# Two PSUM banks as two tiles instead of halves of one, in a fused attention and mixing kernel

## The chip, the core and the metric

The program runs on one core of one Trainium2 chip. The metric is device microseconds of one execution; lower is better.

## What is computed

A causal window attention (8 batches, 8 heads, 576 positions, 64 channels a head, window 128, a linear bias by distance) gives x, 8 batches of 576 x 512. Then each batch goes through a mixing layer:

```python
scores = scale * np.matmul(q, k.transpose(0, 1, 3, 2))
scores = np.where(mask, scores + bias[None], -1000000000.0)
attn = np.exp(scores - np.max(scores, axis=-1, keepdims=True))
attn = attn / (np.sum(attn, axis=-1, keepdims=True) + 1e-09)
x = np.matmul(attn, v)                      # then heads side by side: (8, 576, 512)
theta = x @ w_theta
y = np.einsum('ts,bsd->btd', w_tok_r, x * np.cos(theta)) + np.einsum('ts,bsd->btd', w_tok_i, x * np.sin(theta))
u = x + y
out = u + np.maximum(u @ w_ch, 0.0)
```

## The kernel before

The work is cut into steps. A step belongs to one engine and has an estimated cost; `Plan.__call__` notes which buffers it reads and writes. `Plan.order` simulates all steps with these costs several times, lets a list of numbers (`NUDGES`) disturb the priorities, and gives one fixed order. `Plan.run` emits the instructions in that order, so that every engine's queue, the DMA queue of SP among them, is laid out before the program runs. Where the plan leaves TensorE (PE) idle, `spin` fills the time with short matmuls on a constant tile (L365), whose result nobody reads.

Per pair of heads there are scores on PE (L613), a biased minimum on VectorE (DVE, L637), an exponential on ScalarE (ACT, L642), a transpose of the weights, and the product with the values (`attend`, L672). The first seven pairs (`early_pair`, L711) transpose their weights on PE into the tile `m_ps` (L720) and copy them out with ACT (L723); later pairs split them into two halves of 16 bits and transpose them by DMA. Then, per batch:

- `turn` (L748) computes theta (matmuls L793, L798 and L802 into the tiles `t_psa` and `t_psb`), sine and cosine (ACT, L824 and L826; the tables of sine and exponential are exchanged by a table load) and z = x cos, x sin in two parts of 16 bits.
- `mix` (L894) makes y: for two halves of the positions and four blocks of channels one group of 27 matmuls of 288 columns (L907), issued in three parts of nine, sums into one bank. DVE drains the bank into `xtf` (L913), ACT and DVE make u from that (L917, L920).
- `channels` (L925) multiplies u by w_ch: eight groups of 12 matmuls (L941) a batch, each drained by ACT with the ReLU (L951; tile `u_spare`), then added (L954 or L958) and written out (L960).

There are thus 64 groups of `mix` and 65 of `channels` (the last group of the last batch is cut in two). They take turns in two banks of PSUM. These banks are the two halves of one tile:

```python
a_ring, t_ring = banks("a_ps", 2), banks("t_ps", 2)      # L356: two tiles each
m_both = psum.tile([128, 2, 512], F32, name="m_ps")      # L357: one tile
m_ring = Ring([m_both[:, k] for k in range(2)])          # L358: its halves
```

The plan counts the halves as two buffers. The semaphores that the instructions wait for come from a layer below, which follows tiles. `t_psa` and `t_psb`, `a_psa` and `a_psb` are tiles of their own, used by the same rule of taking turns.

Of the kernel before, what the change touches and what calls it, by code (L numbers as in the profile page):

```python
# [52 lines left out]
while RAD * 0.5 > math.pi:  # L53
# [16 lines left out]
ROUNDS = 6  # L70
SELF = {"DVE": 0.115, "ACT": 0.13, "POOL": 0.1}
NUDGES = (
# [6 lines left out]
)  # L79


# [207 lines left out]
def attn_moe_kernel(ctx: ExitStack, tc: tile.TileContext, qt, kt, vx, wth, wtok, wch, band, out):  # L289
# [10 lines left out]
    def banks(name, n):  # L300
        return Ring([psum.tile([128, 512], F32, name=f"{name}{chr(97 + k)}") for k in range(n)])
# [51 lines left out]
    xp_ring = ring("xp", 2, [128, 2, 512], F16)  # L353

    s_ring = Ring([psum.tile([128, 2, 512], F32, name="s_ps")])
    a_ring, t_ring = banks("a_ps", 2), banks("t_ps", 2)  # L356
    m_both = psum.tile([128, 2, 512], F32, name="m_ps")  # L357
    m_ring = Ring([m_both[:, k] for k in range(2)])  # L358
    first_ring = ring("first", 2, [64, 2, 64], F32)

    def spin(tile, count):
# [240 lines left out]
    def scores(p, weights):  # L602
        qr, kr = raw_qk.pop(p)
        mx_buf, first = mx_ring.take(), first_ring.take()
        mx = mx_buf.tile.rearrange("p (e i) -> p e i", e=2)
        for group in range(2):
            ps, sb = s_ring.take(), sb_ring.take()

            def multiply(group=group, ps=ps):

                def part(e, at, q0, k0, kn, to):
                    rows = slice(64 * e, 64 * e + 64)
                    nc.tensor.matmul(ps.tile[at:at + 64, e, to:to + kn], qr.tile[rows, q0:q0 + 64],  # L613
                                     kr.tile[rows, k0:k0 + kn], start=True, stop=True)
                for j in range(2):
                    c = 2 * group + j
                    k0, to = 128 * c, KEYS * j
                    qa, qb = 64 + k0, 128 + k0
                    if c == 0:
                        for e in range(2):  # L620
                            part(e, 0, 0, 0, 64, 2 * KEYS)
                    part(0, 0, qa, k0, 128, to)
                    part(0, 64, qb, k0, KEYS, to)
                    if c == 0:
                        part(1, 0, qa, k0, 128, to + 64)
                    else:
                        part(1, 0, qa, k0 - 64, KEYS, to)
                    part(1, 64, qb, k0, 128, to + 64)
                    part(0, 0, qa, max(k0 - 64, 0), 64, to + 128)
                    if c == 0:  # L630
                        part(1, 0, qa, 0, 64, to)
                    part(1, 64, qb, k0 + 128, 64, to)
            plan("PE", pe(950 if group == 0 else 790), multiply, r=[(qr, 0), (kr, 0)], w=[(ps, 0)])
            whole = []

            def least_of(out, source, h, at, kn, least, r, w):
                plan("DVE", (0.08 + kn * 1.03e-3, 0.13), lambda: nc.vector.tensor_tensor_reduce(  # L637
                    out=out, in0=source, in1=bands[:out.shape[0], h, at:at + kn], scale=-0.125, scalar=3.0e38, op0=ALU.add,
                    op1=ALU.min, accum_out=least), r=[(ps, 0), (band_buf, h)] + r, w=w)

            def expose(out, source, kn, least, r, w):
                plan("ACT", (0.187 + kn * 0.833e-3, 0.15), lambda: nc.scalar.activation(  # L642
                    out, source, AF.Exp, bias=least, scale=-1.0), r=r, w=w, table="exp")
            for j in range(2):
                c = 2 * group + j
                for e in range(2):
                    at, h = 2 * KEYS * j + KEYS * e, (2 * p + e) % H
                    part, least, key, most = sb.tile[:, at:at + KEYS], mx[:, e, c:c + 1], (sb, (j, e)), (mx_buf, (e, c))
                    least_of(part, ps.tile[:, e, KEYS * j:KEYS * j + KEYS], h, 0, KEYS, least, [], [key, most])
                    expose(part, part, KEYS, least, [most], [key])  # L650
                    whole.append(key)
                    if c == 0:
                        out, least, most = first.tile[:, e], mx[:64, e, 4:5], (mx_buf, (e, 4))
                        least_of(out, ps.tile[:64, e, 2 * KEYS:2 * KEYS + 64], h, 64 + 64 * (h % 2), 64,
                                 least, [], [(first, e), most])
                        expose(part[:64, 128 - 128 * e:192 - 128 * e], out, 64, least, [most, (first, e)], [key])
            if p < EARLY:
                weights[group] = sb, whole
                continue
            hl, pt = hl_ring.take(), pt_ring.take()  # L660
            hi, lo = (hl.tile[:, a * 4 * KEYS:(a + 1) * 4 * KEYS] for a in range(2))
            plan("ACT", (0.78, 0.15), lambda hi=hi, sb=sb: nc.scalar.activation(
                hi, sb.tile, AF.Copy, scale=2.0 ** PEXP), r=whole, w=[(hl, "h")])
            plan("DVE", (0.87, 0.13), lambda hi=hi, lo=lo, sb=sb: nc.vector.scalar_tensor_tensor(
                out=lo, in0=sb.tile, scalar=2.0 ** PEXP, in1=hi, op0=ALU.mult, op1=ALU.subtract),
                r=whole + [(hl, "h")], w=[(hl, "l")], port=True)
            turned = pt.tile.bitcast(F16).rearrange("p (n q) -> p n q", q=128)
            plan("SP", (1.9, 2.0, 0.0), lambda hl=hl, turned=turned: nc.sync.dma_start_transpose(
                out=turned, in_=hl.tile), r=[(hl, "h"), (hl, "l")], w=[(pt, 0)])
            weights[group] = pt, [(pt, 0)]  # L670
# [40 lines left out]
    def early_pair(p, weights, x_buf):  # L711
        vb, k, zs = group_v[p // GROUP], p % GROUP, group_scale[p // PAIRS_OF]
        turned = []
        for group in range(2):
            pt, halves = pt_ring.take(), [m_ring.take() for _ in range(2)]
            sb, read = weights[group]

            def multiply(sb=sb):
                for n in range(6):
                    nc.tensor.transpose(m_both[:, n // 3, n % 3 * 128:n % 3 * 128 + 128],  # L720
                                        sb.tile[:, n * 128:n * 128 + 128], ident)
            plan("PE", pe(6 * 112), multiply, r=read, w=[(half, 0) for half in halves])
            plan("ACT", (0.65, 0.15), lambda pt=pt: nc.scalar.copy(  # L723
                pt.tile.rearrange("p (a n) -> p a n", a=2), m_both[:, :, :384]), r=[(half, 0) for half in halves],
                w=[(pt, 0)])
            turned.append(pt)
        accs = [a_ring.take() for _ in range(2)]

        def block(c, t, a):
            at = (c % 2 * 3 + t) * 128  # L730
            return turned[c // 2].tile[:, at:at + 128]
        plan("PE", pe(1900), lambda: attend(accs, block, [(0, vb.tile[:, k], 65)]),
             r=[(pt, 0) for pt in turned] + [(vb, 0)], w=[(acc, 0) for acc in accs])
        for e, acc in enumerate(accs):
            finish(2 * p + e, acc, x_buf, zs.tile[:, 1:2], [(zs, 1)], 1.0e-9)

    def late_pair(p, weights, x_buf):
        buf = split_values(p)
        vh, vl = buf.tile
        turned = [weights[g][0].tile.bitcast(F16).rearrange("p (a n q) -> p a n q", a=2, q=128) for g in range(2)]  # L740
        accs = [a_ring.take() for _ in range(2)]
        plan("PE", pe(1500), lambda: attend(
            accs, lambda c, t, a: turned[c // 2][:, a, c % 2 * 3 + t], [(0, vh, 65), (0, vl, 64), (1, vh, 65)]),
            r=[(buf, "h"), (buf, "l")] + [(weights[g][0], 0) for g in range(2)], w=[(acc, 0) for acc in accs])
        for e, acc in enumerate(accs):
            finish(2 * p + e, acc, x_buf, None, [], 1.0e-9 * 2.0 ** PEXP)
# [347 lines left out]
```

## Time and profile before

| | us |
|---|---|
| median of 3 runs (lowest, highest) | 649.73 (647.93, 650.14) |
| the profiled execution | 651.64 |
| its span, first to last instruction | 649.9 |
| PE busy (share of the span) | 587.1 (90%) |
| DVE busy | 489.6 (75%) |
| ACT busy | 478.4 (74%) |
| mean granted clock of PE | 0.99 of full |

Busy times overlap, so they are not added. PE's busy time holds the spins. The first mixing group starts 98.9 us into the span. After that the program runs in batches: while `mix` and `channels` of one batch are on PE, the attention of the next is on ACT and DVE; the last batches have only mixing left.

### The profile page before, as it was taken

The numbers are of one execution on the slowest core, as the hardware profiler recorded it, in microseconds if no ns is written. First come the engines' busy times: TensorE is split into PE (matmuls) and PEld (weight loads), VectorE is DVE, ScalarE is ACT, GpSimd is POOL, SyncE is SP. The second block draws the span as 40 slices with busy tenths as digits, with TensorE's granted clock in tenths as the row PEclk, the third lists the DMA queues.
The fourth block names the chain that finished last, engine by engine and source line by source line (L and its number), as shares of the span: only waits on it lengthen the run. The fifth ranks groups of instructions, "written<-read, shape, count | busy, mean of one in ns | idle before, by whom it ended". The sixth has DMA issues, their size and how long they took to land.

```text
span 649.9 us, 18290 instructions
## 1 busy us (share of the span) xinstructions
PE 587.1 (90%) x7442; PEld 438.4 (67%) x7442; DVE 489.6 (75%) x1523; ACT 478.4 (74%) x890; POOL 155.5 (24%) x135
## 2 busy tenths in 40 slices
PE   9999999989899978899799888989999988987885
PEld 8899867766676756667667665757676656665653
DVE  5999999889779974899569886888879845433222
ACT  5999999599899977988789978768876653342112
POOL 0002110034441246202840044102700441050000
PEclk9999999999999989999999999989999999999999
DMA  8976421988597657565667576293527122001002
GB/s 309 408 285 191 142 79 49 186 184 170 141 217 109 103 130 155 152 154 123 141 144 140 123 139 143 95 165 76 99 66 120 14 71 66 9 10 65 1 1 73
DMA packets 140101, 82.02 MB, mean 126 GB/s; under 512 B 119152, under 2 KB 127600, under 8 KB 140016
## 3 DMA queue, kind: packets, MB, share of 16 engines
q1 hardware_dynamic: 140016, 80.84, 52.3%
q8 instruction: 58, 0.95, 0.6%
q14 instruction: 27, 0.22, 0.1%
HBM read 42.29 MB, written 9.44 MB: 80 GB/s over the span
## 4 chain that ended last, share of the span: by engine, by line
PE 60%; ACT 15%; issue 10%; DVE 6%; DMA 6%; POOL 1%; SPq 0%; DVEq 0%; ACTq 0%; POOLq 0%
PE m_ps L907 23%; PE m_ps L941 14%; PE t_psa L793 5%; PE s_ps L613 5%; PE t_psb L793 4%; ACT u_spare L951 4%; DMA xpa<-hlxa 2%; PE a_psa L365 2%; DMA ptd<-hlb 2%; PE a_psa L678 1%; DVE xtfb L913 1%; PE a_psb L678 1%; PE a_psa L695 1%; ACT L642 1%; ACT sba L642 1%
## 5 line engine op out<-in xcount | busy, mean ns | idle before, releaser
L907 PE MATMUL m_ps<-wtk_hi,z_hi 128*128 128x288 f16 x576 | 165.0, 286 | 22.6 <-DVE xtfb L913 9.8
L907 PE MATMUL m_ps<-wtk_hi,z_lo 128*128 128x288 f16 x576 | 164.7, 286 | 0.0
L907 PE MATMUL m_ps<-wtk_lo,z_hi 128*128 128x288 f16 x576 | 164.6, 286 | 0.0
L907 PEld LDWEIGHTS <-z_hi 128*128 128x128 f16 x1152 | 109.3, 98 | 58.5 <-issue 28.8
L941 PE MATMUL m_ps<-u,wch 128*128 128x288 f16 (+1 forms) x780 | 105.8, 289 | 26.8 <-ACT u_spare L951 23.7
L941 PEld LDWEIGHTS <-wch 128*128 128x128 f16 x780 | 75.7, 99 | 54.4 <-issue 33.0
L951 ACT ACTIVATE u_spare<-m_ps,fixed 128x288 f32<-128x288 f32 (+1 forms) x65 | 32.0, 494 | 52.0 <-PE m_ps L941 47.0
L409 POOL TENSOR_TENSOR z_lo<-wch_held,z_hi 128x512 f16<-128x512 f32 x32 | 40.6, 1282 | 109.9 <-ACT z_hi L835 60.1
L907 PEld LDWEIGHTS <-z_lo 128*128 128x128 f16 x576 | 56.3, 98 | 14.3
L857 POOL TENSOR_TENSOR hlxa<-x_sba,hlxa 128x512 f16<-128x512 f32 (+1 forms) x12 | 17.2, 1435 | 126.4 <-ACT hlxa L856 126.4
L917 ACT ACTIVATE u<-xtfb,fixed 128x288 f16<-128x288 f32 x32 | 16.8, 529 | 38.5 <-DVE xtfb L913 38.4
L365 PEld LDWEIGHTS <-white 128*128 128x128 bf16 x474 | 40.4, 101 | 4.5 <-issue 1.7
L913 DVE SCALAR_TENSOR_TENSOR xtfb<-m_ps,fixed,xtfb 128x288 f32<-128x288 f32 x32 | 16.4, 513 | 34.9 <-PE m_ps L907 31.5
L365 PE MATMUL a_psa<-white 128*128 128x187 bf16 x405 | 39.5, 252 | 2.0 <-DVE a_psa L378 1.5
L642 ACT ACTIVATE sba<-sba,fixed 128x192 f32<-128x192 f32 x88 | 36.4, 447 | 6.2 <-DVE fixed L637 6.2
L642 ACT ACTIVATE sbc<-sbc,fixed 128x192 f32<-128x192 f32 x84 | 34.6, 447 | 3.1 <-DVE fixed L637 2.8
L917 ACT ACTIVATE u<-xtfa,fixed 128x288 f16<-128x288 f32 x32 | 16.7, 529 | 26.6 <-DVE xtfa L913 26.5
L642 ACT ACTIVATE sbb<-sbb,fixed 128x192 f32<-128x192 f32 x84 | 34.1, 446 | 2.7 <-DVE fixed L637 2.4
L793 PEld LDWEIGHTS <-xpa 128*128 128x128 f16 x192 | 18.7, 99 | 24.8 <-DMA xpa<-hlxa 4.5
L637 DVE CUSTOM_DVE_ANT_0 sba<-s_ps,bands 128x192 f32<-128x192 f32 x88 | 28.3, 346 | 7.1 <-PE s_ps L613 7.1
L913 DVE SCALAR_TENSOR_TENSOR xtfa<-m_ps,fixed,xtfa 128x288 f32<-128x288 f32 x32 | 16.2, 512 | 22.6 <-PE m_ps L907 18.9
L793 PEld LDWEIGHTS <-xpb 128*128 128x128 f16 x192 | 18.7, 99 | 20.8 <-issue 1.1
(402 smaller groups left out, 1499.6 us busy)
## 6 DMA issues: line engine op xcount, KB each, us to landing
vba<-in_vx_dram SPq DMA_DIRECT2D x6, 845.0 KB, 5.8
out_dram<-xtfa SPq DMA_DIRECT2D x32, 144.0 KB, 2.0
out_dram<-xtfb SPq DMA_DIRECT2D x31, 144.0 KB, 1.8
vbb<-in_vx_dram SPq DMA_DIRECT2D x5, 845.0 KB, 6.3
vbc<-in_vx_dram SPq DMA_DIRECT2D x5, 845.0 KB, 5.6
kra<-in_kt_dram SPq DMA_DIRECT2D x11, 288.0 KB, 3.0
qra<-in_qt_dram SPq DMA_DIRECT2D x11, 288.0 KB, 3.5
krb<-in_kt_dram SPq DMA_DIRECT2D x11, 288.0 KB, 3.9
```

The costliest lines, as they stand in the source:

```text
L365: nc.tensor.matmul(spun, white[:, :128], white[:, :spun.shape[-1]], start=True, stop=True)
L409: plan(engine, cost, lambda: on.tensor_tensor(out=out, in0=whole, in1=part, op=ALU.subtract), r=r, w=w, port=True)
L613: nc.tensor.matmul(ps.tile[at:at + 64, e, to:to + kn], qr.tile[rows, q0:q0 + 64], kr.tile[rows, k0:k0 + kn], start=True, stop=True)
L637: plan("DVE", (0.08 + kn * 1.03e-3, 0.13), lambda: nc.vector.tensor_tensor_reduce(out=out, in0=source, in1=bands[:out.shape[0], h, at:at + ...
L642: plan("ACT", (0.187 + kn * 0.833e-3, 0.15), lambda: nc.scalar.activation(out, source, AF.Exp, bias=least, scale=-1.0), r=r, w=w, table="exp")
L793: nc.tensor.matmul(t_ps, a[:, c * 128:c * 128 + 128], w[:, c, :], start=(k == 0 and c == 0), stop=(k == len(prods) - 1 and c == 3))
L857: plan("POOL", pool(512), lambda: nc.gpsimd.tensor_tensor(out=lo, in0=x, in1=hi, op=ALU.subtract), r=every + [(hlx, "h")], w=[(hlx, "l")])
L907: nc.tensor.matmul(y.tile[:, :HALF], z[:, c, m * 128:m * 128 + 128], w[:, c, cs], start=(part == 0 and j == 0 and a == 0), stop=(part == 2 ...
L913: plan("DVE", (0.425, 0.13), lambda y=y, at=at: nc.vector.scalar_tensor_tensor(out=at, in0=y.tile[:, :HALF], scalar=back, in1=at, op0=ALU. ...
L917: plan("ACT", (0.43, 0.15), lambda m=m, cs=cs, at=at: nc.scalar.activation(u_hi[:, m, cs], at, AF.Copy, scale=share), r=[(xtf, ("y", m, hf ...
L941: nc.tensor.matmul(o.tile[:, :n], w[:, c, e * 128:e * 128 + 128], u[:, c, cs], start=(k == 0), stop=(k == 11))
L951: plan("ACT", (0.15 + n * 0.835e-3, 0.15), lambda: nc.scalar.activation(r.tile[:, :n], o.tile[:, :n], AF.Relu, scale=zs.tile[:, 7:8]), r=[ ...
```

## The change

Three edits. `m_ps` becomes two tiles, `m_psa` and `m_psb`, of one bank each. An early pair's six transposes per group become two steps of three, each into its own bank, and each with its own copy of 384 columns by ACT (14 copies of 768 columns become 28 of 384). The costs of five steps and the list of numbers are others, so the plan gives another order.

```diff
-    a_ring, t_ring = banks("a_ps", 2), banks("t_ps", 2)
-    m_both = psum.tile([128, 2, 512], F32, name="m_ps")
-    m_ring = Ring([m_both[:, k] for k in range(2)])
+    a_ring, t_ring, m_ring = banks("a_ps", 2), banks("t_ps", 2), banks("m_ps", 2)
...
-            plan("PE", pe(950 if group == 0 else 790), multiply, r=[(qr, 0), (kr, 0)], w=[(ps, 0)])
+            plan("PE", pe(930 if group == 0 else 830), multiply, r=[(qr, 0), (kr, 0)], w=[(ps, 0)])
...
-            pt, halves = pt_ring.take(), [m_ring.take() for _ in range(2)]
+            pt = pt_ring.take()
             sb, read = weights[group]
-
-            def multiply(sb=sb):
-                for n in range(6):
-                    nc.tensor.transpose(m_both[:, n // 3, n % 3 * 128:n % 3 * 128 + 128],
-                                        sb.tile[:, n * 128:n * 128 + 128], ident)
-            plan("PE", pe(6 * 112), multiply, r=read, w=[(half, 0) for half in halves])
-            plan("ACT", (0.65, 0.15), lambda pt=pt: nc.scalar.copy(
-                pt.tile.rearrange("p (a n) -> p a n", a=2), m_both[:, :, :384]), r=[(half, 0) for half in halves],
-                w=[(pt, 0)])
+            for j in range(2):
+                half, at = m_ring.take(), 2 * KEYS * j
+
+                def multiply(sb=sb, half=half, at=at):
+                    for n in range(3):
+                        nc.tensor.transpose(half.tile[:, n * 128:n * 128 + 128],
+                                            sb.tile[:, at + n * 128:at + n * 128 + 128], ident)
+                plan("PE", pe(340), multiply, r=[key for key in read if key[1][0] == j], w=[(half, 0)])
+                plan("ACT", (0.40, 0.15), lambda pt=pt, half=half, at=at: nc.scalar.copy(
+                    pt.tile[:, at:at + 2 * KEYS], half.tile[:, :2 * KEYS]), r=[(half, 0)], w=[(pt, j)])
...
-        plan("PE", pe(1900), lambda: attend(accs, block, [(0, vb.tile[:, k], 65)]),
-             r=[(pt, 0) for pt in turned] + [(vb, 0)], w=[(acc, 0) for acc in accs])
+        plan("PE", pe(2450), lambda: attend(accs, block, [(0, vb.tile[:, k], 65)]),
+             r=[(pt, j) for pt in turned for j in range(2)] + [(vb, 0)], w=[(acc, 0) for acc in accs])
...
-        plan("PE", pe(1500), lambda: attend(
+        plan("PE", pe(1340), lambda: attend(
```

Of the list of numbers, 76 entries before and 51 now, nothing is shown: they have no meaning by themselves. What they and the costs do to the queues is seen in the order of the instructions. In both programs PE has the same matmuls and transposes; the spins are 474 before and 473 now. Ahead of the first mixing group stand 428 and 417 of them; behind the last early pair, 4 and 49. The transposes that are made by DMA are 90 in both (40 of x, for theta, into `xpa` and `xpb`, 50 of the late pairs' weights into `pta` to `ptd`). Table loads on ACT are 42 before and 40 now.

ACT, in the early pairs (ahead of them stand the loads of the weights; L642 is the exponential, L425 and L435 prepare weights, `pta` and `ptb` take the transposed weights). Before:

```order
L723 COPY pta<-m_ps 128x768
L642 ACTIVATE sbb<-sbb,fixed 128x192
L642 ACTIVATE sbc<-sbc,fixed 128x192
L425 ACTIVATE exa<-u_spare 128x512
L435 ACTIVATE u_spare<-u_spare 128x512
L723 COPY ptb<-m_ps 128x768
L425 ACTIVATE exb<-u_spare 128x512
```

and now:

```order
L721 COPY pta<-m_psa 128x384
L421 ACTIVATE exa<-u_spare 128x512
L421 ACTIVATE exb<-u_spare 128x512
L638 ACTIVATE sbb<-sbb,fixed 128x192
L431 ACTIVATE u_spare<-u_spare 128x512
L721 COPY pta<-m_psb 128x384
L638 ACTIVATE sbb<-sbb,fixed 128x192
L721 COPY ptb<-m_psa 128x384
L721 COPY ptb<-m_psb 128x384
```

One copy of both banks has become two copies of one bank, and other work may stand between them.

PE, in the last batch's mixing groups (the semaphore of DVE is called DVE_49). Before:

```order
L907 MATMUL m_ps<-wtk_hi,z_lo 128x288
L907 LDWEIGHTS z_hi
L907 MATMUL m_ps<-wtk_hi,z_hi 128x288 [waits DVE_49]
L907 LDWEIGHTS z_hi
L907 MATMUL m_ps<-wtk_lo,z_hi 128x288
```

and now:

```order
L904 MATMUL m_psa<-wtk_hi,z_lo 128x288
L904 LDWEIGHTS z_hi
L904 MATMUL m_psb<-wtk_hi,z_hi 128x288 [waits DVE_49]
L904 LDWEIGHTS z_hi
L904 MATMUL m_psb<-wtk_lo,z_hi 128x288
```

The instruction that begins a new group waits for DVE in both; the group ahead of it is in the same tile before, and in the other tile now.

## Rows read from the trace of the kernel before

**Rows 1.** Timeline of PE, 300 to 330 us: start, us, engine, line, operation [idle before <-releaser].

```profile
314.75 3.10 PE L941 MATMUL m_ps<-u,wch 128*128 128x288 f16 x24 [0.92 <-ACT u_spare L951]
318.44 1.63 PE L941 MATMUL m_ps<-u,wch 128*128 128x288 f16 x12 [0.59 <-ACT u_spare L951]
```

**Rows 2.** Timeline of ACT, 295 to 330 us.

```profile
317.89 0.50 ACT L951 ACTIVATE u_spare<-m_ps,fixed 128x288 f32<-128x288 f32 x1 [1.07 <-PE m_ps L941]
```

**Rows 3.** Chain of waits, 560 to 650 us: start, us, what.

```profile
581.74 1.64 PE m_ps L941 x12
583.40 0.51 ACT u_spare L951
583.91 0.04 issue
583.96 1.64 PE m_ps L941 x12
```

**Rows 4.** Waits of PE, 450 to 650 us: us in total, times, longest (all rows).

```profile
PE m_ps L941 <- ACT u_spare L951: 10.8, 18, 0.7
PE m_ps L907 <- DVE xtfb L913: 6.0, 9, 1.0
PE m_ps L907 <- ACT u_spare L951: 3.2, 5, 0.7
PE m_ps L907 <- DVE xtfa L913: 3.0, 5, 0.6
PE m_ps L941 <- DVE xtfb L913: 1.8, 3, 0.6
PE m_ps L941 <- DVE xtfa L913: 0.6, 1, 0.6
```

**Rows 5.** Waits of PE, 95 to 450 us (the four smallest are left out).

```profile
PE m_ps L941 <- ACT u_spare L951: 13.0, 14, 2.9
PE t_psa L793 <- DMA xpa<-hlxa: 4.2, 2, 2.6
PE m_ps L907 <- DVE xtfb L913: 3.8, 6, 0.7
PE m_ps L907 <- DVE xtfa L913: 3.7, 5, 1.8
PE m_ps L907 <- ACT u_spare L951: 2.8, 4, 1.0
PE a_psa L678 <- DMA ptd<-hlb: 1.3, 1, 1.3
```

**Rows 6.** Windows: us, PE, PEld, DVE, ACT, POOL busy (count), PEclk, DMA share, GB/s.

```profile
95.00:450.00 355.00, 324.03 (x4484) 234.81 (x4483) 295.26 (x931) 302.38 (x554) 102.25 (x86) 0.99 0.65 138
450.00:650.00 200.00, 170.41 (x1588) 122.65 (x1586) 108.19 (x254) 90.96 (x166) 44.96 (x37) 0.99 0.23 50
```

**Rows 7.** Window of the early stage, the same columns.

```profile
20.00:95.00 75.00, 74.23 (x1124) 63.73 (x1124) 73.53 (x278) 72.98 (x149) 7.46 (x5) 1.00 0.64 219
```

**Rows 8.** Groups of ACT by form: busy us, mean ns of one | idle before.

```profile
L951 ACT ACTIVATE u_spare<-m_ps,fixed 128x288 f32<-128x288 f32 x63 | 31.3, 497 | 51.0 <-PE m_ps L941 46.1 <-PE m_ps L907 2.3 <-POOL hlxa L857 1.2
...
L723 ACT COPY pta<-m_ps 128x768 f32<-128x768 f32 x4 | 3.2, 794 | 0.0
```

**Rows 9.** Groups of ACT: the table loads of the exponential.

```profile
L642 ACT ACT_TABLE_LOAD x21 | 26.9, 1283 | 1.0 <-PEq L1081 0.7
```

**Rows 10.** Timeline of PE, 236 to 258 us: one stretch of 24 matmuls.

```profile
238.92 5.92 PE L941 MATMUL m_ps<-u,wch 128*128 128x288 f16 x24 [2.88 <-ACT u_spare L951]
```

**Rows 11.** Windows around the two falls of the clock, columns as above.

```profile
238.00:245.00 7.00, 5.92 (x24) 3.49 (x24) 3.98 (x17) 3.11 (x8) 1.67 (x2) 0.51 0.37 87
...
429.00:433.00 4.00, 4.00 (x12) 1.51 (x11) 3.60 (x7) 2.75 (x5) 1.15 (x1) 0.57 0.79 149
```

**Rows 12.** The page, section 5: the spins, out<-in xcount | busy us, mean ns | idle before.

```profile
L365 PE MATMUL a_psa<-white 128*128 128x187 bf16 x405 | 39.5, 252 | 2.0 <-DVE a_psa L378 1.5
```

**Rows 13.** DMA issues: line, xcount, median us to landing.

```profile
ptd<-hlb SPq DMA_TRANSPOSE x13, 5.4
```

10 rows, old and new, of the table NUDGES are left out of this document.

## The prediction

> **What bounds the kernel now.** I read the windows first, to see which engine is full where, then PE's waits, then the timelines and the chain, to see what a wait is made of. From 95 us to 450 us PE is busy for 324.0 of 355 us, ACT for 302.4 (85%) and DVE for 295.3 (83%); from 450 us on PE is busy for 170.4 of 200 us and ACT for 91.0 [rows 6]. So PE is the bound from 95 us to the end, and what counts is where it stands still. The lists of its waits answer that: nearly all are waits of a mixing matmul for a drain of `m_ps`, 41 from 450 us on, 25.4 us in total [rows 4], and 14 + 6 + 5 + 4 = 29 before, 13.0 + 3.8 + 3.7 + 2.8 = 23.3 us [rows 5].
>
> There are two banks, so a group should wait for the drain of the group before last, which is long over. The rows show something else. In the chain of the last channels every step is the same: 12 matmuls, the drain by ACT (0.51 us), 0.04 us, and the next 12 matmuls, 2.22 us from one group to the next [rows 3]. That is one bank's rhythm. And a drain waits too: at 314.75 us two groups run without a gap, 24 matmuls in 3.10 us [rows 1], so the first was ready after some 1.6 us, at 316.4; its drain started only at 317.89, right behind the second, after ACT had stood idle for 1.07 us [rows 2]. Reader and writer of one half wait for whoever touched the tile last. `t_psa` and `t_psb`, which are two tiles under the same rule of turns, appear in neither list as something PE waits for; their only row is a wait for a DMA [rows 4, 5].
>
> **The change, term by term,** against the profiled execution, 651.6 us; it lies 1.9 us above the median of the runs, 649.7, and I subtract that at the end.
>
> *What a wait costs.* A lone group of 12 takes 1.63 us, two in a row 3.10 [rows 1]: the second adds 1.47. So a group that has to wait loses the idle time and also 0.16 us, the end of its predecessor, which it could have overlapped. The chain agrees: 2.22 - 1.47 = 0.75, against an idle time of 0.59 in the timeline [rows 1, 3].
>
> *From 450 us on:* 25.4 + 41 x 0.16 = 32.0 us. With two tiles a group waits for the drain of the group before last; that drain ends 0.6 us after its group [rows 3], while the group between takes 1.47 us, so the cover is 0.9 us, and ACT and DVE are about half idle here [rows 6]. Taken whole: -32.0. Bounds: -32.0, and -25.4 if the overlap is not won.
>
> *From 95 to 450 us:* at most 23.3 + 29 x 0.16 = 27.9 us. Here a wait lasts 0.80 us on average against 0.62 in the tail (25.4 / 41). The difference, 29 x 0.18 = 5.2 us, is a drain that came late because ACT or DVE, which take their work in order, had something else ahead; the longest wait is 2.9 us [rows 5]. Two tiles give such a drain more time, but nothing makes it earlier, so I leave these 5.2 us out. Some 3 us more I leave for waits that come up anew: a PE that runs faster meets an ACT that is as busy as before, 302.4 us of work in 335 us instead of 355, 90%. In the early stage ACT stands at 73.0 of 75 us, 97% [rows 7], so this density can be reached by a fixed order. Taken: -19.5. Bounds: 0 and -27.9.
>
> *The clock.* It falls twice to half, 1.2 GHz: at 238 us, behind 2.88 us in which PE waited for a drain of `m_ps`, and at 429 us, behind a wait for a DMA of 2.6 us [rows 5, 10, 11]. At half clock 24 matmuls take 5.92 us instead of 3.10. The first fall should go with its wait: -2.8; the second stays. Bounds: 0 and twice that.
>
> *Copies.* 14 copies of 768 columns, 794 ns, become 28 of 384, which no row has. Between bounds of half a whole copy (397 ns, sum 0) and a whole one (28 x 794 - 14 x 794 = +11.1 us) I take the line through the two drains by ACT that have rows, 497 ns for 288 columns and 794 for 768 [rows 8]: 556 ns, so 28 x 0.556 - 14 x 0.794 = +4.5 us. The list in the VectorE: DVE Perf Modes page of the Trainium skill, section The TRN2 errata, counts 172 cycles and one a column, at 1.2 GHz, for ScalarE out of PSUM; by it an estimate for 384 columns is 463 ns, and the term would be +1.8 us, 2.7 less; for 768 columns it gives 783 ns, and the row has 794. Two table loads less, 1.283 us each [rows 9], take off 2.6. ACT is full in this stage, so the rest counts whole: +1.9. Bounds: -2.6 and +8.5. The split also lets a bank's second user start earlier; I cost that at nothing, since PE fills this stage with spins.
>
> *Order and spins.* One spin less in total; 45 more lie in the later part, 39.5 / 405 = 0.098 us each [rows 12], 4.4 us, and 11 fewer ahead of the first group. They stand where the plan has PE idle, behind scores, so what hides them is the wait that they fill; if that is not there, they cost up to 4.4 us, which is in the range. All other PE work is the same.
>
> Sum: 651.6 - 32.0 - 19.5 - 2.8 + 1.9 = 599.2; less 1.9 for the median: **597 us**.
>
> **The rivals.**
>
> *ACT takes over in the middle.* In-order queues may not go denser than they are now: at ACT's present 85% nothing of the middle is won, and the time is 651.6 - 32.0 + 1.9 - 1.9 = 620; at 88% the stage takes 302.4 / 0.88 = 343.6 us, 11.4 less, and the time is 608. For it: ACT and DVE are both above 80% there and hand work to each other. Against: the 97% of the early stage.
>
> *Everything is won.* All 27.9 us, and the copies at their lower bound: 651.6 - 32.0 - 27.9 - 2.8 - 2.6 - 1.9 = 584. For it: no other wait in the middle is large; only 5.5 us are for DMA [rows 5].
>
> *The transposes by DMA become the bound, and it is slower.* 90 of them feed PE through one queue, and one takes up to 5.4 us (median) to land [rows 13]; the DMA engines are busy for 65% of the middle [rows 6]. A faster PE and an order that was laid out anew may stand before a tile that has not landed. Today that happens three times, 5.5 us, 1.83 each. The gain of 52.4 us is gone from the 29th such wait on; if every third transpose came late, 32 in all with the three of today among them, the 29 new ones would take 53 us, and beyond that it is slower: at every second one, 42 new waits, 597 + 77 = 674. Against: three in ninety is far from one in two.
>
> *The clock falls oftener.* PE's short gaps between groups did not bring it down: 70 waits, and a fall only behind 2.88 and 2.6 us of standing still. If the new order had one more such fall in each of seven batches, it would cost 7 x 2.8 = 20 us: 617. The page TensorE: Matmul & The Clock Gate of the Trainium skill, section A second HAM failure mode: psum-queue depth-cycling, tells of a kernel that cycled through banks and whose clock went up and down because of small gaps between groups; by that rule the two banks would be a danger, and the trace, with its 0.99 [rows 6], doesn't bear it out.
>
> *The change does nothing:* the two tiles are still waited for as one. Then all stays near 650. `t_psa` and `t_psb` speak against it.
>
> **How the numbers follow.** My forecast, 589 to 607: 0.60. ACT in the middle, 608 to 620: 0.22. Everything won, under 589: 0.10. Clock: 0.02. DMA: 0.04, on the slower side. No effect: 0.02. A difference of 0.3%, 2 us, is what runs of this kernel can tell from none. Faster: 0.60 + 0.22 + 0.10 + 0.02 = 0.94; same 0.02; slower 0.04. The range runs from the fully won middle to the middle not won, 585 to 620; some of the lowest case and the last two lie outside.
>
> **What would show it.** Right: in the list of PE's waits the rows of `m_ps` shrink from 49 us to under 8; the last channels stand 1.47 us apart; ACT is at 90% in the middle; no fall of the clock behind a drain. The first group at about 99 us shows the copies right; past 102 us they were dearer. Wrong: waits of PE for ACT, DVE or POOL in the middle of more than 10 us (ACT's case), many rows of PE behind DMA (the transposes), or the 2.22 us rhythm unchanged (no effect).

## The result, and the profile after

The changed kernel takes 594.0 us (median of 4 runs, 593.79 to 595.61), the kernel before, measured beside it, 649.93 us (647.93 to 650.66). The ratio is 0.9149, with a 95% interval of 0.9123 to 0.9175: 56 us less. The forecast was 597 us, with a range of 585 to 620.

The page of the changed kernel, its profiled execution at 595.61 us, sections 1 and 2 (the clock row has 40 slices of the span):

```profile
span 593.8 us, 18307 instructions
PE 576.4 (97%) x7441; PEld 436.7 (74%) x7441; DVE 499.2 (84%) x1523; ACT 475.1 (80%) x902; POOL 162.5 (27%) x135
...
PEclk9999999999999999999999999999999999999999
```

PE has about the same busy time as before (576.4 us, 587.1 before) in a span that is 56 us shorter. What went is idle time, and the two falls of the clock: no slice stands below 9. The windows of the changed kernel (columns as in [rows 6, 7]):

```profile
20.00:95.00 75.00, 73.47 (x1094) 61.16 (x1095) 73.14 (x292) 72.93 (x161) 6.65 (x5) 1.00 0.65 211
95.00:450.00 355.00, 344.77 (x4783) 253.34 (x4775) 319.53 (x977) 319.90 (x596) 123.41 (x98) 1.00 0.69 145
450.00:600.00 150.00, 139.67 (x1346) 105.04 (x1344) 94.86 (x203) 71.35 (x125) 31.58 (x25) 0.99 0.23 54
```

In the middle PE is busy for 344.8 of 355 us where it had 324.0, and ACT for 319.9, which is 90% where it had 85% [rows 6]. So the same queues hold a denser load. The waits of PE from 95 to 450 us (all rows but four small ones of `s_ps` and `a_psa`, and one of a `t_psb`), in us in total, times, longest:

```profile
PE m_psb L938 <- ACT u_spare L948: 2.1, 2, 1.9
PE m_psa L904 <- DVE xtfa L910: 1.7, 3, 0.9
PE t_psa L790 <- DMA xpb<-hlxb: 1.4, 1, 1.4
PE t_psa L790 <- DMA xpa<-hlxa: 1.0, 1, 1.0
...
PE m_psa L938 <- ACT u_spare L948: 0.3, 1, 0.3
```

and from 450 us to the end, both rows that there are:

```profile
PE t_psb L790 <- DMA xpa<-hlxa: 0.4, 1, 0.4
PE m_psb L938 <- DVE xtfb L910: 0.3, 1, 0.3
```

The waits for a bank of mixing sums are 2.1 + 1.7 + 0.3 + 0.3 = 4.4 us. Before they were 25.4 and 23.3 us [rows 4, 5]. The chain of the last channels has lost its rhythm of matmuls, drain, matmuls [rows 3] (columns: start, us, what):

```profile
578.59 1.47 PE m_psa L938 x12
580.06 1.47 PE m_psb L938 x12
581.53 1.47 PE m_psa L938 x12
583.00 1.47 PE m_psb L938 x12
```

Each group follows the one before it after 1.47 us in place of 2.22, and no drain is in the chain: while ACT empties one bank, PE fills the other.

### The profile page after: what moved, and what is told of

Read it like the earlier page. It is cut to its first block, busy times and chain, and to the rows that moved or that the text cites. A ratio compares the mean times of both kernels' runs of the same rounds, so it can differ in the third digit from the quotient of the medians.

```text
span 593.8 us, 18307 instructions
## 1 busy us (share of the span) xinstructions
PE 576.4 (97%) x7441; PEld 436.7 (74%) x7441; DVE 499.2 (84%) x1523; ACT 475.1 (80%) x902; POOL 162.5 (27%) x135
## 4 chain that ended last, share of the span: by engine, by line
PE 49%; DVE 15%; ACT 14%; DMA 13%; issue 6%; POOL 3%; SPq 1%; POOLq 0%; DVEq 0%; ACTq 0%
PE m_psb L904 11%; PE m_psa L904 10%; PE m_psa L938 5%; PE m_psb L938 5%; PE t_psa L790 4%; PE t_psb L790 4%; PE s_ps L609 4%; DMA xpa<-hlxa 4%; DMA xpb<-hlxb 2%; DMA ptb<-hlb 2%; DMA krc<-in_kt_dram 1%; POOL z_lo L405 1%; PE a_psa L674 1%; ACT sbb L638 1%; DMA u_spare<-in_wth_dram 1%
## 5 line engine op out<-in xcount | busy, mean ns | idle before, releaser
L938 PEld LDWEIGHTS <-wch 128*128 128x128 f16 x780 | 74.3, 98 | 24.0 <-issue 4.2
L904 PE MATMUL m_psa<-wtk_hi,z_hi 128*128 128x288 f16 x288 | 82.5, 286 | 1.8 <-DVE xtfa L910 1.7
L904 PE MATMUL m_psb<-wtk_hi,z_hi 128*128 128x288 f16 x288 | 82.6, 287 | 0.0
L904 PE MATMUL m_psb<-wtk_hi,z_lo 128*128 128x288 f16 x288 | 82.4, 286 | 0.0
L904 PE MATMUL m_psb<-wtk_lo,z_hi 128*128 128x288 f16 x288 | 82.4, 286 | 0.0
L904 PE MATMUL m_psa<-wtk_hi,z_lo 128*128 128x288 f16 x288 | 82.4, 286 | 0.0
L904 PE MATMUL m_psa<-wtk_lo,z_hi 128*128 128x288 f16 x288 | 82.3, 286 | 0.0
L405 POOL TENSOR_TENSOR z_lo<-wch_held,z_hi 128x512 f16<-128x512 f32 x32 | 43.7, 1380 | 82.3 <-ACT z_hi L832 66.5
L938 PE MATMUL m_psb<-u,wch 128*128 128x288 f16 (+1 forms) x384 | 51.6, 284 | 2.5 <-ACT u_spare L948 2.1
L938 PE MATMUL m_psa<-u,wch 128*128 128x288 f16 (+1 forms) x396 | 53.2, 284 | 0.3 <-ACT u_spare L948 0.3
L854 POOL TENSOR_TENSOR hlxa<-x_sba,hlxa 128x512 f16<-128x512 f32 (+1 forms) x12 | 15.7, 1306 | 122.8 <-ACT hlxa L853 122.8
L790 PEld LDWEIGHTS <-xpb 128*128 128x128 f16 x192 | 18.4, 98 | 22.3 <-DMA xpb<-hlxb 2.0
```

The costliest lines, as they stand in the source:

```text
L405: plan(engine, cost, lambda: on.tensor_tensor(out=out, in0=whole, in1=part, op=ALU.subtract), r=r, w=w, port=True)
L790: nc.tensor.matmul(t_ps, a[:, c * 128:c * 128 + 128], w[:, c, :], start=(k == 0 and c == 0), stop=(k == len(prods) - 1 and c == 3))
L854: plan("POOL", pool(512), lambda: nc.gpsimd.tensor_tensor(out=lo, in0=x, in1=hi, op=ALU.subtract), r=every + [(hlx, "h")], w=[(hlx, "l")])
L904: nc.tensor.matmul(y.tile[:, :HALF], z[:, c, m * 128:m * 128 + 128], w[:, c, cs], start=(part == 0 and j == 0 and a == 0), stop=(part == 2 ...
L938: nc.tensor.matmul(o.tile[:, :n], w[:, c, e * 128:e * 128 + 128], u[:, c, cs], start=(k == 0), stop=(k == 11))
```

## The experiments

"Old order" means the order of the instructions of the kernel before, "new order" that of the changed kernel. Each ratio is against the kernel before, run beside it on the same chip. A granted clock of a run is the mean of PE's over its span, 1.0 being full.

### One part of the change alone: tiles, order

The first kernel has the two tiles in the old order, instruction for instruction; an early copy is two copies next to each other.

```diff
-    m_both = psum.tile([128, 2, 512], F32, name="m_ps")
-    m_ring = Ring([m_both[:, k] for k in range(2)])
+    m_ring = banks("m_ps", 2)
...
-                    nc.tensor.transpose(m_both[:, n // 3, n % 3 * 128:n % 3 * 128 + 128],
+                    nc.tensor.transpose(halves[n // 3].tile[:, n % 3 * 128:n % 3 * 128 + 128],
...
+                for k in range(2):
+                    nc.scalar.copy(pt.tile[:, k * 384:k * 384 + 384], halves[k].tile[:, :384])
```

> The order of the kernel before, instruction for instruction, with the two banks as two tiles; only an early pair's copy becomes two copies, one right behind the other. Theory (the wait on the whole tile cost the time, the order is only what the planner laid out): 650 - 32 in the tail - 20 to 28 in the middle - 2.8 for the clock + 2 for the copies, so 590 to 602 us, PE's waits for m_ps under 8 us, no fall of the clock behind a drain. Rival (the new order brought the gain): 640 to 652 us. Rival (half and half): about 620 us.

Measured: 602.64 us (594.56 to 603.60), ratio 0.9233 (0.9153 to 0.9312). That is 0.6 us above the expected range, and two signs missed: over the whole span PE waits 9.8 us for `m_psa` and `m_psb`, not under 8, and the clock did fall behind a drain, as shown below. The second kernel has the new order, and the two banks as halves of one tile again.

```diff
-    a_ring, t_ring, m_ring = banks("a_ps", 2), banks("t_ps", 2), banks("m_ps", 2)
+    a_ring, t_ring = banks("a_ps", 2), banks("t_ps", 2)
+    m_both = psum.tile([128, 2, 512], F32, name="m_ps")
+    m_ring = Ring([m_both[:, k] for k in range(2)])
```

> The changed kernel, instruction for instruction, with the two banks again as halves of one tile. Theory: the waits come back; 640 to 660 us, PE's waits for m_ps 45 us or more, the last channels 2.2 us apart, the first mixing group some 2 us later than with two tiles, since the split copies and transposes wait for each other too. Rival (the order brought the gain): 594 to 605 us. Half and half: about 620 us.

Measured: 642.57 us (642.09 to 643.70), ratio 0.9891 (0.9841 to 0.9942). The kernel before stood at 650.27 us beside both. So the tiles alone give 650.27 - 602.64 = 47.6 us (48 in the repetition below) and the order alone 7.7; on top of the order the tiles give 642.57 - 594.0 = 48.6, on top of the tiles the order gives 8.6. The two add up, and the tiles are six parts in seven. The waits of PE in the second kernel, whole span, the six largest:

```profile
PE m_ps L940 <- ACT u_spare L950: 20.9, 30, 1.9
PE m_ps L906 <- DVE xtfb L912: 7.3, 12, 0.7
PE m_ps L906 <- ACT u_spare L950: 6.5, 10, 0.9
PE m_ps L906 <- DVE xtfa L912: 5.4, 9, 0.9
PE m_ps L940 <- DVE xtfb L912: 2.4, 4, 0.6
PE m_ps L940 <- DVE xtfa L912: 2.3, 3, 1.1
```

That is 44.8 us in 68 waits for `m_ps`, nearly the 48.7 us of the kernel before: the order alone does not remove them. 44.8 + 68 x 0.16 = 55.7 us is what the prediction's price would make of them; the tiles gave 48.6 here, 87% of it. The chain of its last channels has the drain between the groups again, 2.22 us from one group to the next,

```profile
630.09 1.64 PE m_ps L940 x12
...
631.76 0.51 ACT u_spare L950
...
632.31 1.65 PE m_ps L940 x12
```

and in the first kernel, whose order is the old one, it is gone:

```profile
586.24 1.47 PE m_psa L942 x12
587.71 1.47 PE m_psb L942 x12
```

Since the first kernel has the old order, its instructions can be set against those of the kernel before one by one. The first mixing group starts 0.4 us earlier. The matmul that started at 450.07 us starts at 432.75, 17.3 us earlier, and the last matmul of the channels ends 47.9 us earlier. So the middle gave 16.9 us and the tail 30.6 (17.9 and 30.6 in the repetition below).

Why did the first kernel stop 8 us short? Its waits of PE from 95 to 450 us, the five largest:

```profile
PE m_psa L942 <- ACT u_spare L952: 4.3, 1, 4.3
PE t_psa L794 <- DMA xpa<-hlxa: 4.2, 2, 2.7
PE m_psb L942 <- ACT u_spare L952: 2.4, 4, 1.2
PE a_psa L677 <- DMA ptd<-hlb: 1.8, 1, 1.8
PE m_psb L908 <- DVE xtfa L914: 0.7, 1, 0.7
```

One long wait for a drain by ACT is left, and it is longer than any before: 4.3 us. The timeline of ACT at this place:

```profile
229.16 0.85 ACT L661 ACTIVATE hla<-sbc 128x768 f16<-128x768 f32 x1 [3.12 <-DMA ptc<-hla]
...
232.61 1.28 ACT L641 ACT_TABLE_LOAD   x1
...
235.07 0.50 ACT L952 ACTIVATE u_spare<-m_psa,fixed 128x288 f32<-128x288 f32 x1
```

and that of PE:

```profile
227.41 1.63 PE L942 MATMUL m_psa<-u,wch 128*128 128x288 f16 x12
...
235.63 3.04 PE L942 MATMUL m_psa<-u,wch 128*128 128x288 f16 x12 [4.31 <-ACT u_spare L952]
```

Read from the top: ACT must write a late pair's weights into `hla` and stands for 3.12 us, since a transposing DMA still reads `hla`. Its queue is in order, so casts, a table load and exponentials come next, and the drain of the group that PE ended at 229.04 starts at 235.07. PE needs that bank, stands for 4.31 us, and then runs the next 12 matmuls in 3.04 us where 1.63 is usual, at half clock (1.2 GHz in place of 2.4). In the kernel before ACT stood for 1.69 us at the same instruction,

```profile
231.47 0.84 ACT L662 ACTIVATE hla<-sbc 128x768 f16<-128x768 f32 x1 [1.69 <-DMA ptc<-hla]
```

PE at the same place for 2.88 us, and its clock fell behind that [rows 10, 11].

In this trace of the first kernel the clock fell three times in the middle, not twice as in the kernel before. The windows around the falls:

```profile
233.00:241.00 8.00, 5.37 (x27) 3.56 (x27) 6.66 (x19) 6.99 (x16) 5.32 (x6) 0.57 0.37 88
362.00:367.00 5.00, 5.00 (x97) 3.75 (x94) 2.93 (x12) 3.75 (x8) 2.30 (x2) 0.66 0.54 116
410.00:415.00 5.00, 4.40 (x13) 1.71 (x14) 4.37 (x10) 1.91 (x3) 1.15 (x1) 0.66 1.00 203
```

The first is the one just told. Ahead of the other two stand the waits for the transposing DMAs of the list above, 1.8 us for `ptd` and 2.7 us for `xpa`. In the kernel before the fall at 429 us had such a wait ahead of it; at the place of the one near 363 us PE waited for 1.3 us and the clock stayed up [rows 5].

### The lateness of ACT: a third buffer

To take the cause away, and nothing else, the first kernel got a third physical buffer behind `hla` and `hlb`; the plan still counts two, so the order stays.

```diff
+    hl_real = hl_tiles + [place("hlc", [128, 8 * KEYS], F16)]
+    hl_count = [0]
...
             hl, pt = hl_ring.take(), pt_ring.take()
+            hl.tile = hl_real[hl_count[0] % 3]
+            hl_count[0] += 1
```

> Two tiles in the order of before, with the third buffer behind hla and hlb. Theory (in the old order ACT stands behind a transposing DMA near 229 us, the drain of m_ps behind it comes late, PE waits 4.3 us and its clock falls; the third buffer takes the first link away): PE's wait of 4.3 us is gone, no fall of the clock near 233 us, 594 to 598 us. Rival (the drain is late because of ACT's own work): 600 to 604 us, the wait still there.

Measured: 596.68 us (593.50 to 599.52), ratio 0.9185 (0.9153 to 0.9218). Beside it, on the same chip, the first kernel ran again:

> Two tiles in the order of before once more, beside the kernel with the third buffer on the same chip. Theory: 593 us where the clock does not fall, 600 to 604 us where it does, in the same order of instructions. Rival (the executions differ by something else): times that do not follow the granted clock.

Measured: 601.59 us (599.02 to 604.32), ratio 0.9267 (0.9237 to 0.9296). No execution kept its clock at 1.0 (0.991 to 0.996), so the 593 us that were expected for one are not tested, and the times do not follow the clock closely: 599.02 us at 0.994, 601.53 at 0.996. The intervals of the two kernels don't meet: the third buffer is worth 4.9 us in the old order. ACT in the kernel with three buffers, the same instruction:

```profile
224.53 0.83 ACT L665 ACTIVATE hla<-sbc 128x768 f16<-128x768 f32 x1
```

Nothing is waited for there any more. PE at the drain that it waited for, in the kernel with three buffers

```profile
230.97 1.63 PE L946 MATMUL m_psa<-u,wch 128*128 128x288 f16 x12 [0.23 <-ACT u_spare L956]
```

and in the first kernel's second run:

```profile
237.60 3.04 PE L942 MATMUL m_psa<-u,wch 128*128 128x288 f16 x12 [4.36 <-ACT u_spare L952]
```

The wait is 0.23 us in place of 4.36, and the clock stays up there. So the chain from the DMA's hold on `hla` by way of ACT's queue to PE and its clock is shown at this place, not only argued. The other two falls of the first kernel are not explained by it. The repetition's trace has them again, behind waits of 1.92 and 2.53 us; in the trace with three buffers PE waits at the same two instructions for 1.67 and 2.48 us, and the clock stays at 1.0.

The same buffer in the changed kernel, with the changed kernel run again beside its repetition:

> The changed kernel in its order, with a third buffer behind hla and hlb, so that ACT's split of a late pair need not wait for the DMA that transposes the pair before last. Theory (what is left of waits in the middle is ACT held up in its queue by such a DMA; in the changed kernel that is 6.4 us of ACT's idle time, little of it on PE's path): 590 to 594 us. Rival (nothing of it reaches PE): 594 us, the same. Rival (the transposes collide more when they start earlier): 596 us or more.

Measured: 592.48 us (592.17 to 593.62), ratio 0.9125 (0.9101 to 0.9149).

> The changed kernel once more, beside the one with the third buffer on the same chip. Theory: 593 to 595.5 us, as before.

Measured: 592.77 us (592.21 to 595.17), ratio 0.9125 (0.9100 to 0.9150), 0.2 us under the expected range.

> The changed kernel with the third buffer behind hla and hlb once more. Theory (the third buffer takes away waits of ACT that PE hardly feels): 0.5 to 2 us less than the changed kernel in the same call. Rival: no difference, within 0.5 us either way.

Measured: 592.63 us (592.06 to 594.18), ratio 0.9123 (0.9099 to 0.9148). No difference: in the new order the third buffer buys nothing, and no version here beats the changed kernel. It is not that ACT no longer waits for these DMAs. Over the whole span it waits for `hla` and `hlb` 15.3 us in the changed kernel, in 11 waits, and 13.2 us in the first kernel; with the third buffer one wait of 3.6 us is left in the new order, and the time is the same. In the changed kernel the timeline of ACT has, for one,

```profile
406.54 0.84 ACT L658 ACTIVATE hlb<-sbb 128x768 f16<-128x768 f32 x1 [2.34 <-DMA ptb<-hlb]
```

but the window around it shows PE busy throughout, at full clock:

```profile
403.00:410.00 7.00, 7.00 (x71) 3.91 (x57) 5.33 (x12) 4.25 (x6) 1.15 (x1) 1.00 0.96 138
```

The new order has 24 matmuls of theta and then a mixing group there, which need nothing from ACT at this moment. So the order does not make ACT punctual; at this place it puts other work on PE while ACT is late.

### The spins

The plan's spins behind the early pairs were taken out of the changed kernel (`FILL` tells the plan how much idle time of PE to fill).

```diff
-FILL, FULL = 0.8, 130.0
+FILL, FULL = 0.0, 130.0
```

> The changed kernel without the 49 spins behind the last early pair; all other queues are the same. Theory (they fill a wait for ACT and DVE that is there): 593 to 595 us, the same, with PE idle where they stood. Rival (PE would have been ready): 4.4 us less, 589 to 591 us. Rival (they keep the clock up): a fall of the clock in the second batch and 597 us or more.

Measured: 594.31 us (591.59 to 596.94), ratio 0.9146 (0.9093 to 0.9198): no difference from the changed kernel's 594.0. In its profile the clock fell once in the stretch that the spins had filled; the window there, without the spins

```profile
150.00:200.00 50.00, 42.07 (x622) 30.11 (x617) 43.32 (x148) 45.75 (x88) 24.71 (x20) 0.97 0.75 168
```

and in the changed kernel:

```profile
150.00:200.00 50.00, 46.52 (x699) 34.46 (x697) 44.43 (x150) 47.63 (x90) 24.64 (x20) 1.00 0.77 176
```

PE is busy for 4.4 us less in it, and ends no earlier; the granted clock of the four runs is 0.994 to 0.997. The spins fill waits, and what they keep up, the clock, is not needed at that place.

### The new steps with the old list of numbers

Is any order good that the planner finds? The changed kernel with `NUDGES` of the kernel before (76 entries in place of 51, nothing else):

> The changed kernel with the list of numbers of the kernel before, so another order of the same steps and waits. Theory (the tiles bring the gain, the numbers some us): 595 to 610 us. Rival (the numbers decide): 620 us or more.

Measured: 626.97 us (626.13 to 630.02), ratio 0.9657 (0.9610 to 0.9704). That is 33 us above the changed kernel, and it missed what was expected by more than 15 us. The plan put 248 more spins into this program (7689 matmuls in place of 7441), so it was run without the late ones, with `FILL` at 0.0 as above:

> The new steps with the old list of numbers, without the spins behind the last early pair. Theory (the 33 us that this order costs are waits of PE for ACT and DVE, laid out by the plan and filled with spins): 620 to 630 us, and PE's list of waits names DVE and ACT for 20 us or more. Rival (the spins themselves stand in the way): 605 to 615 us.

Measured: 627.84 us (625.99 to 631.36), ratio 0.9672 (0.9638 to 0.9705). The spins are not the loss. The first five batches are: from one batch's first mixing group to the next they take 82.2, 80.7, 74.3, 73.7 and 66.7 us with the spins, together 377.6, and in the changed kernel 73.9, 71.0, 71.9, 66.1 and 65.3, together 348.2. The two intervals behind them agree to 0.2 us. The waits of PE without the spins, 115 to 450 us, the four largest:

```profile
PE m_psb L940 <- ACT u_spare L950: 3.9, 1, 3.9
PE s_ps L611 <- DVE fixed L635: 3.5, 2, 2.1
PE m_psb L906 <- DVE xtfb L912: 3.0, 1, 3.0
PE a_psa L676 <- DMA ptd<-hlb: 2.7, 1, 2.7
```

These are waits for ACT, DVE and a DMA of up to 3.9 us each; one of 3.3 us for DVE lies at 112 us, just ahead of the window. Over the whole span PE waits 24 us for ACT and DVE, as expected, where the changed kernel has 10. The clock is the other part: without the spins it is granted at 0.95 from 95 to 450 us (0.97 over the span in all four runs), where the changed kernel has 1.00 and this order with the spins 0.99. That is 0.05 x 355 = 18 us at most, by estimate. So the spins kept the clock up here and took about as much time as that was worth. Which step of that order makes the waits long was not taken apart.

## Why the prediction held, step by step

**The mechanism** was right. Both parts of its reasoning, that the halves of one tile are waited for as one, and that this is nearly all of what PE waits for, stand on the second kernel: with halves the 2.22 us rhythm and the waits are there in either order, with two tiles the rhythm and most of the waits are gone in either order.

**What a wait costs, and the tail.** Forecast -32.0 us, measured -30.6 in the same order. The idle time alone was 25.4 us, so the lost overlap of 0.16 us a wait is real, and nearly all of it came back.

**The middle and the clock.** Together -22.3 was forecast, and -16.9 came in the old order. The step that failed there is "the first fall should go with its wait": the wait stayed, because the drain was late behind a held-up ACT; only some 1.0 us of it was the tile's, by estimate, the time in which PE in the kernel before stood for the second of two drains (they end at 237.87 and 238.86 us). It grew from 2.88 to 4.3 us, since PE gets there 4.7 us earlier and the drain starts only 2.3 us earlier, and the clock fell behind it. The prediction had left 5.2 us in the middle for drains that come late and 3 for new waits, and 8.4 us in 8 waits for a bank stayed: the right thing at the right size. But it did not look for the place, which was the very wait that it took for the cause of the first fall [rows 10]. So in the old order the term of the waits was nearly right and the term of the clock was wrong in its sign. At the prediction's price the waits for a bank fell from 23.9 us in 30 (with a row of 0.6 that [rows 5] leaves out) to 8.4 in 8, which makes 15.5 + 22 x 0.16 = 19.0 us; the waits for transposing DMAs grew from 5.5 to 6.0; and three falls in place of two cost up to 1.7 us more, where 2.8 less was forecast. 19.0 - 0.5 - 1.7 = 16.8, and 16.9 was measured. In the new order the step came true, since no drain is that late: no fall, and 8.6 us less than in the old order. In the old order the third buffer alone gave 4.9. What is left then, 596.68 - 592.48 = 4.2 us with three buffers in both orders, lies in those executions of the old order in which the clock fell: the two with a granted clock of 1.0 took 593.50 and 594.17 us, the four from 0.991 to 0.997 took 595.8 to 599.5, and the changed kernel, at 0.997 to 1.0, 592.2 to 595.6. Which waits brought those falls stays open, since these executions have no trace; the two waits for transposing DMAs at which the first kernel's clock fell are the nearest candidates, and that is argued, not shown. One execution of the first kernel kept its clock at 1.0 and took 594.56 us; the kernel before did so once, at 646.79. The difference, 52.2 us, is near the sum without its clock term, 32.0 + 19.5 - 1.9 = 49.6, by one execution of each. That agrees with terms for the waits of about the right size, and a clock that depended on the order.

**The copies.** Forecast +1.9 us with a half copy at 556 ns. The groups of ACT by form, in the changed kernel (four of eight; columns as in [rows 8]):

```profile
L721 ACT COPY ptb<-m_psa 128x384 f32<-128x384 f32 x4 | 1.9, 472 | 0.8 <-PE m_psa L718 0.8
...
L721 ACT COPY pta<-m_psa 128x384 f32<-128x384 f32 x4 | 1.9, 464 | 0.0
L721 ACT COPY pta<-m_psb 128x384 f32<-128x384 f32 x4 | 1.8, 461 | 0.0
...
L721 ACT COPY ptc<-m_psb 128x384 f32<-128x384 f32 x3 | 1.4, 452 | 0.0
```

Over all 28 the mean is 464 ns, so this term was mis-sized: the work is 14 x (2 x 0.464 - 0.794) = +1.9 us where +4.5 was taken, and -0.7 with the two table loads. The line had been drawn through a ReLU of 288 columns and a copy of 768, two different operations. The estimate from the Trainium skill, page VectorE: DVE Perf Modes, section The TRN2 errata, 463 ns, agrees with the rows. None of it is seen on the path: in the first kernel, with the same copies, the first mixing group starts 0.4 us earlier than before, and in its repetition 0.6 later, although ACT is full there. In the changed kernel it starts at 101.33 us (before 98.9), and at 100.8 in the second kernel, which has one tile and was expected to be later by 2 us; that missed. Six traces in which the instructions up to there are those of the changed kernel, but for the tile, lie between 99.3 and 101.6 us, four of the old order between 98.6 and 99.6. So the later start belongs to the new order and to a spread of 2 us between executions, not to the copies, and the sign that the prediction named ("past 102 us they were dearer") would have misled.

**Order and spins.** Nothing was forecast for the spins, and the runs without them show nothing. For the order itself the prediction had no term; it was worth 8.6 us with the two tiles, of which 22.3 - 16.9 = 5.4 stood in the sum under the middle and the clock.

**The rivals.** ACT taking over in the middle, 608 to 620 us, did not come: ACT went to 90%, the share that was forecast, and DVE likewise, 319.5 of 355 us. But it is not far away. The same steps under the old list take 627 us with waits of that very kind, so the density needs an order that is fitted to it. The transposes by DMA cost PE 1.4 + 1.0 + 0.4 us in the rows above, less than the 4.2 + 1.3 before [rows 5]; it is ACT that they hold up. In the changed kernel's traces the clock did not fall oftener; in the old order with two tiles it did, three times in place of two. The rule on bank cycling in the Trainium skill, page TensorE: Matmul & The Clock Gate, section A second HAM failure mode: psum-queue depth-cycling, was put to the test by the second kernel: 68 waits for a bank, 0.66 us each in the mean, with a granted clock of 0.999 to 1.0 in all four runs. There the many gaps between groups did not bring the clock down, the longest of them 1.9 us. In the other traces most falls stand behind a single wait of 1.8 to 4.4 us, but one (at 383 us, with the old list of numbers) behind two of 1.0 and 0.8 us, and waits of 1.9, 2.0 and 2.5 us passed without a fall.

**The sum.** 597 forecast, 594.0 measured, 592.8 in the repetition. The errors were small and partly cancelled: copies 2.6 us too dear, the tail 1.4 too good, and a new order that did more than the old one in the middle. That the sum came within 3 us is in part luck: its terms price the two tiles, by which alone 602.64 and 601.59 us were measured, and the order's 8.6 us had no term of their own.

## What to carry to other kernels

In this program two buffers that are views of one tile are one buffer for the waits. Where a ring of two shows the rhythm of a ring of one (work, drain, work), look at how the buffers are declared before looking at the engines. Price such a wait as the idle time plus the lost overlap at the end of the group before it, and where a drain is late by more than its own duration, read what stands ahead of it in the queue of the draining engine. A buffer that an in-order engine must get back from a DMA can hold up everything behind it, TensorE and its clock included, and giving it one more buffer or putting other work on the waiting engine are two cures for the same thing, so they don't add.

## What was not expected of the hardware

- Executions of one program can lie 9 us apart, and the granted clock goes with it in the main: the first kernel took 594.56 us at a granted clock of 1.0 and 603.27 at 0.989, the kernel with three buffers in that order 593.50 at 1.0 and 599.52 at 0.991. The changed kernel, with two buffers and with three, at 0.996 to 1.0, stays within 592.1 to 595.6. The loss is larger than the mean clock alone makes it (1.1% of 603 us is 6.6 us), so waits should belong to it, as the 4.3 us ahead of one fall; executions without a trace don't show them. Not all of the spread is the clock: the changed kernel took 592.21 and 595.17 us, both at 1.0, and its traced executions differ before the first mixing group.
- A fall of the clock does not always cost time. Without the late spins PE's clock fell at 179 us, behind a wait of 2.57 us for DVE, and the median stayed the same: PE was idle for 8 of the 50 us around it. With the third buffer in the new order it fell at 408 us, behind a wait of 2.06 us for DVE, in an execution of 592.42 us; in the repetition PE waited 2.01 us at the same instruction and the clock stayed up.
- A list of numbers that was fitted to one set of steps costs 33 us on a set that differs by 14 split copies and five costs.
